# Spacing and placing the conversions of w2, and moving three other loads, in a fused attention and Fourier-mixing kernel

## The chip, the cores and the metric

The kernel runs on one core of one Trainium2 chip. The metric is the device time of a run in microseconds, the median of several runs. The engines are named as in the profile: PE (TensorE matmuls; PEld is its weight load), DVE (VectorE), ACT (ScalarE), POOL (GpSimd) and SP (SyncE, which here only issues DMAs). [...]

## The reference

Bucketed attention comes first, then a mixing block with a two-layer MLP. All data is fp32; the wide inputs arrive as 64-bit floats, which the kernel itself brings to 32 bits.

```python
# attention: B, H, S, D = 4, 8, 768, 64
q_bucket = sum((q @ proj > 0) * 2**arange(6))      # k_bucket likewise
scores = where(q_bucket[:, None] == k_bucket[None, :], q @ k.T / 8, -1e9)
x = softmax(scores) @ v                            # heads side by side: (4, 768, 512)
# mixing block
u = x + real(fft2(x))                              # over the sequence, then over the channels
un = (u - mean(u)) / sqrt(var(u) + 1e-6)
out = u + maximum(un @ w_ch1, 0) @ w_ch2           # 512 -> 2048 -> 512
```

## The kernel before, in words

**Batches and stages.** The four batches are pipelined. While `attention(b)` runs for batch b, the generator `mix(b - 1)` is advanced a few steps after each step of attention, so the PE finds transform and MLP products between the score and value products. `attention(b)` takes four pairs of heads, each in six chunks of 128 keys: score products (L894), the exponential on ACT (L905, tile `pk`), for pairs past the fifth the bucket mask on DVE (L919), the value products (L930), and on DVE the running sum of weights (`acc`, L1007). `mix(b)` does two foldings on DVE, six steps with the channel transform's table `ch` (PE L1122), four with the sequence transform's table `sq` (PE L1151, then `x<-x,A` and `x<-x,B` on DVE, L1165), and then `mlp7(b)`.

**The MLP.** `mlp7` computes both matrix products by a seven-product scheme over 2x2 blocks. For the first product, `quarters(f)` forms four combinations of blocks of `w1` on DVE (L1224 to L1227, tile `tq`) and stores all seven operands to DRAM for the later batches (`ad`, L1229 and L1230, on SP). `inner(half)` then does four groups of seven products (`h_p`, L1426), with evacuations and additions on ACT and DVE (L1448 to L1477). `outer7(b, half, ...)` does the second product (`o`, L1306) with the seven operands of `w2` in `right7`. Each MLP has two halves: inner(0), outer7(0), inner(1), outer7(1).

**Where the weights come from.** Both weights are fetched in slices of 512 KB as 64-bit numbers and brought to 32 bits by `Arrival.convert`, which calls `narrow`: DVE L639 and L643, ACT L647, DVE L649 or twice L652, then ACT L654 and L655 for a range check. When a conversion is done, `convert` fetches the slice that will use the same raw buffer. `weights1` has seven raw buffers and runs during `attention(0)`; it also asks for the second pair's q, k and v, by `load(1)`, after its second fetch. `weights2` has two raw buffers only (`zt2`), and POOL issues its fetches (L693). It converts eight slices for the first half and eight for the second; after every second conversion it forms four sums (L1272 to L1275), and after eight it stores the seven operands (`bd`, L1277, on SP).

**What sets the order.** Batch 0's attention is ordered as written (`manual_schedule`). From there on a scheduler orders each engine's queue. `issue_after(ins)` makes an instruction stand behind `ins` in the queue of that engine, and adds no wait. `weights2` is advanced inside `mix(0)`, which runs beside `attention(1)`: by `after(n, one, two)` from step n of mix(0) on, in three of every five steps, and in the second half by the loop in `mlp7` in three of every four steps:

```python
other = after(2 + NT, other, islice(arrival2, HF + 1))     # NT = 6, HF = 8
if b == 0 and half and i % 4 < 3:
    next(arrival2, None)
```

The two tables `ch` and `sq` are asked for on SP just before attention(0) begins, behind the first seven slices of `w1`.

Of the kernel before, what the change touches and what calls it, by code (L numbers as in the profile page):

```python
# [485 lines left out]
def _main(  # L486
# [188 lines left out]
    def centre(f, avg):  # L675
        for c in range(NDC):
            w = w1[:, c, f : f + WC]
            nc.vector.tensor_tensor(w, w, avg, op=ALU.subtract)

    class Arrival:  # L680

# [29 lines left out]
    def weights1():  # L711
        slices = [
            (w1[:, c, f : f + WC], moe_w_ch1[c * P : (c + 1) * P, f : f + WC])
            for f in range(0, DFF, WC)
            for c in range(NDC)
        ]
        zt = wt([P, 3, 2 * WC], F32, "z", "zraw1", 1)
        ft = wt([P, 12, WC], F32, "F", "fraw", 1)
        raws = [zt[:, i] for i in range(3)] + [
            ft[:, i : i + 2].rearrange("p i w -> p (i w)") for i in range(0, 8, 2)  # L720
        ]
        arrival = Arrival(slices, raws, 0, nc.sync)
        for i in range(arrival.depth):
            arrival.fetch(i)
            if i == 1:
                load(1)
        yield
        half = None
        for i in range(len(slices)):
            arrival.convert(i, ft[:, 8 + i % 4].bitcast(I32))  # L730
            yield
            if half:
                centre(half[0], next(half[1]))
                half = None
# [168 lines left out]
    def weights(pk, g, ps):  # L903

        nc.scalar.activation(  # L905
            pk[:, g, :, 0:HALF], ps[:, :, 0:HALF], AF.Exp, scale=SCALE
        )

    def weigh(n, c, pss):

        qb, kb = preps[n][2:]
        pk = pks[npk[0] % NPK]
        npk[0] += 1
        for g in range(2) if n >= TWO else ():
            weights(pk, g, pss[g])
        if kb is not None:
            for h in range(2):
                w = pk[:, :, h, 0:HALF]
                nc.vector.scalar_tensor_tensor(  # L919
                    w, qb[:, h].rearrange("p (g s) -> p g s", g=2), kb[:, h, c : c + 1], w,  # L920
                    op0=ALU.is_equal, op1=ALU.mult,
                )
        return pk
# [181 lines left out]
    def mix(b):  # L1105
# [8 lines left out]
        for par in range(2):  # L1114
            for t in range(NT // 2):
# [12 lines left out]
                for k in kinds:  # L1128
                    nc.scalar.copy(
                        f[:, k, k : hd + 1 - k],  # L1130
                        ps[:, k * (hd + 1) : DM if k else hd + 1],
                    )
# [12 lines left out]
        for j in range(NDC):  # L1145
# [10 lines left out]
            for ps, op in (pa, ALU.add), (pb, ALU.subtract):  # L1156
                for i in range(2):
# [4 lines left out]
                    else:  # L1162
                        f = ps[:, HW : HALF + 1]
                        f = bass.AP(f.tensor, f.offset, [f.ap[0], [HW, 2], [-1, HW]])
                    nc.vector.tensor_tensor(  # L1165
                        u, u, f, op=op if (j < 2) ^ i else ALU.add
# [82 lines left out]
    def weights2():  # L1249
# [14 lines left out]
        for half in range(2):  # L1264
            for i in range(arrival.depth) if half == 0 else ():
                arrival.fetch(i)
            for i in range(HF):
                arrival.convert(half * HF + i)
                yield
# [99 lines left out]
    def mlp7(b):  # L1369
# [7 lines left out]
        if b == 0:  # L1377
# [11 lines left out]
            ss = [s1s[0], spare[3].rearrange("p (r n) -> p r n", n=P)]  # L1389
            quarters(0)  # L1390
        prods = [A11, S2, A12, S1, S3, S4, A22]
# [41 lines left out]
        def inner(half):  # L1433
            for r in range(HF // 2):
# [15 lines left out]
                product(S2, p6)  # L1450
                nc.scalar.copy(c21, p6)  # L1451
                nc.vector.tensor_tensor(c21, c12, c21, op=ALU.add)  # L1452
                yield
# [3 lines left out]
                product(S1, p5)  # L1457
                nc.scalar.copy(c22, p5)  # L1458
                nc.vector.tensor_tensor(c22, c21, c22, op=ALU.add)  # L1459
                yield  # L1460
# [6 lines left out]
                nc.scalar.copy(c12, p5)  # L1467
                nc.vector.tensor_tensor(c12, c21, c12, op=ALU.add)
                nc.scalar.activation(c12, c12, AF.Relu)
                if b and f == 0:  # L1470
# [4 lines left out]
                nc.scalar.copy(sd[1], p7)  # L1475
                nc.vector.tensor_tensor(c21, c21, sd[1], op=ALU.add)
                nc.scalar.activation(c21, c21, AF.Relu)  # L1477
                if b == 0 and r < HF // 2 - 1:
# [4 lines left out]
        for half in range(2):  # L1483
            if b == 0 and half:
                quarters(HF // 2)
            for i, _ in enumerate(inner(half)):
                if b == 0 and half and i % 4 < 3:
                    next(arrival2, None)
# [10 lines left out]
    def after(n, one, two):  # L1499

        for i, _ in enumerate(one):
            if i >= n and (i - n) % 5 < 3:
                next(two, None)
# [7 lines left out]
    next(other)  # L1511
    nc.sync.dma_start(ch, cn["ch"].ap())
    nc.sync.dma_start(sq, cn["sq"].ap())


    ET = mybir.EngineType
    with tc.manual_schedule(engines={ET.PE, ET.DVE, ET.Activation, ET.Pool, ET.SP}):
        for _ in prepare(0):
            pass
        roomy[0] = False  # L1520
        for i, _ in enumerate(attention(0)):
            if i % 5 < 4:
                next(other, None)
# [12 lines left out]
    for b in range(B):  # L1536
# [42 lines left out]
        if b == 0:  # L1579
            zt2 = wt([P, 3, 2 * WC], F32, "z", "zraw2", 1)  # L1580
            arrival2 = weights2()
            other = after(2 + NT, other, islice(arrival2, HF + 1))
    for _ in other:
# [46 lines left out]
```

## Time and profile before

| | |
|---|---|
| median of 3 runs | 1095.56 us (1094.76 to 1096.2) |
| the profiled execution, its own time | 1097.14 us |
| its span, first to last instruction | 1095.2 us |
| PE busy | 1036.7 us, 95% |
| DVE busy | 789.0 us, 72% |
| ACT busy | 500.1 us, 46% |
| POOL busy | 58.3 us, 5% |
| mean granted PE clock | 0.993 |

The stages lie so: batch 0's attention with the conversions of `w1` up to some 115 us; attention(1) beside mix(0) up to some 410 us, with the sixteen conversions of `w2` from 155.8 to 347 us; attention(2) beside mix(1) from there to 670 us, attention(3) beside mix(2) to 922 us, and mix(3) alone to the end. A line of the timeline gives start and duration in us, engine, source line, operation, the tile written and those read, and in brackets how long the engine had stood idle just before and what released it. A row of the windows gives for each engine the busy time in the stretch with the number of instructions, then the granted PE clock, the DMA share and the DMA rate.

### The profile page before, as it was taken

What the parts mean: (1) busy time and instruction counts of PE and PEld (TensorE: products, weight loads), DVE (VectorE), ACT (ScalarE), POOL (GpSimd) and SP (SyncE); (2) the same over time, 40 slices, a digit from 0 to 9 for tenths busy, and PEclk for the clock granted to TensorE, in tenths of its full rate; (3) what the DMA queues carried; (4) which work ended last, traced back from release to release, by engine and by line L of the source; (5) the groups of instructions that cost most, each with busy time, mean ns of one, the idle gap of its engine ahead of it and who ended that gap; (6) DMA issues with size and microseconds to landing.
All of it is one profiled execution on the core that took longest, in us unless ns stands there. A gap on an engine that the chain in (4) does not pass through costs nothing.

```text
span 1095.2 us, 14139 instructions
## 1 busy us (share of the span) xinstructions
PE 1036.7 (95%) x4933; PEld 634.0 (58%) x4933; DVE 789.0 (72%) x1336; ACT 500.1 (46%) x1055; POOL 58.3 (5%) x132
## 2 busy tenths in 40 slices
PE   6989897999989999999999999999999999999997
PEld 3333354446744675545674576645675569768676
DVE  5899968868599978694867776876775875744353
ACT  6988555653276325364426423354415522341430
POOL 0000000002000020010000011001000002100000
PEclk9999899999999999999999999999999999999999
DMA  8744363441056162214063224213123204122401
GB/s 222 225 91 97 60 166 85 149 148 26 20 138 200 55 199 56 51 54 92 15 176 90 63 54 168 44 34 90 27 71 122 78 20 173 52 85 71 141 20 41
DMA packets 175710, 103.13 MB, mean 94 GB/s; under 512 B 129552, under 2 KB 162960, under 8 KB 175632
## 3 DMA queue, kind: packets, MB, share of 16 engines
q1 hardware_dynamic: 169840, 88.65, 30.1%
q0 software_dynamic: 4224, 13.11, 3.8%
q8 instruction: 41, 0.67, 0.3%
q10 hardware_dynamic: 1568, 0.39, 0.2%
q14 instruction: 37, 0.30, 0.1%
HBM read 81.14 MB, written 20.97 MB: 93 GB/s over the span
## 4 chain that ended last, share of the span: by engine, by line
PE 57%; DVE 15%; ACT 4%; issue 3%; DMA 2%; DVEq 0%; ACTq 0%
PE o L1306 23%; PE h_p L1426 18%; PE oo L930 5%; PE sc L894 5%; DVE pk L919 5%; DVE acc L1007 3%; PE cs L1122 2%; DMA zraw<-in_moe_w_ch_dram 2%; PE A L1151 1%; ACT rr L965 1%; ACT pk L905 1%; PE B L1151 1%; PE bits L825 1%; DVE x L1165 1%; DVE w L1318 0%
## 5 line engine op out<-in xcount | busy, mean ns | idle before, releaser
L1306 PE MATMUL o<-w,h 128*128 128x256 f32 x1152 | 258.5, 381 | 1.9 <-DVE w L1318 0.8
L1306 PEld LDWEIGHTS o<-w,h 128*128 128x128 f32 x1152 | 216.8, 190 | 41.7 <-issue 3.5
L905 ACT ACTIVATE pk<-sc 128x768 f32<-128x768 f32 x192 | 146.9, 809 | 94.2 <-PE sc L894 31.3
L1426 PE MATMUL h_p<-x,w 128*128 128x384 f32 x448 | 162.4, 492 | 2.1 <-ACT h L1448 1.7
L894 PE MATMUL sc<-qt,kt 64*128 64x384 f32 x768 | 154.2, 504 | 6.2 <-ACT pk L905 5.9
L919 DVE SCALAR_TENSOR_TENSOR pk<-qb,kb,pk 128x768 f32<-128x768 bf16 x132 | 129.3, 1012 | 34.5 <-ACT pk L905 34.3
L930 PE MATMUL oo<-pk,vn 128*64 128x385 f32 (+1 forms) x768 | 147.8, 495 | 4.9 <-DVE pk L919 4.6
L1426 PEld LDWEIGHTS h_p<-x,w 128*128 128x128 f32 x448 | 82.5, 190 | 67.2 <-issue 6.8
L1007 DVE TENSOR_TENSOR acc<-acc,pk 128x1536 f32<-128x1536 f32 (+1 forms) x72 | 105.9, 1484 | 5.9 <-ACT pk L905 5.4
L1426 PE MATMUL h_p<-w 128*128 128x384 f32 x288 | 106.3, 492 | 3.6 <-ACT w L1463 2.3
L930 PEld LDWEIGHTS oo<-pk,vn 128*64 128x64 f32 x768 | 50.7, 136 | 92.3 <-issue 73.3
L894 PEld LDWEIGHTS sc<-qt,kt 64*128 64x128 f32 x768 | 66.6, 187 | 57.4 <-issue 19.0
L1426 PEld LDWEIGHTS h_p<-w 128*128 128x128 f32 x288 | 53.0, 190 | 45.5 <-ACT w L1475 5.1
L1318 DVE SCALAR_TENSOR_TENSOR w<-o,rs,w 128x256 f32<-128x256 f32 x56 | 26.7, 479 | 42.0 <-PE o L1306 42.0
L1336 ACT COPY tq<-o 128x256 f32<-128x256 f32 x24 | 8.9, 373 | 101.8 <-PE o L1306 101.8
L1306 PE MATMUL o<-w 128*128 128x256 f32 x176 | 42.0, 381 | 0.3 <-DVE w L1318 0.3
L1459 DVE TENSOR_TENSOR h<-h 128x384 f32<-128x384 f32 x32 | 17.7, 553 | 29.5 <-ACT h L1458 29.5
L1452 DVE TENSOR_TENSOR h<-h 128x384 f32<-128x384 f32 x32 | 17.8, 555 | 26.9 <-ACT h L1451 26.8
L1306 PEld LDWEIGHTS o<-w 128*128 128x128 f32 x176 | 33.0, 190 | 6.8 <-issue 1.1
L1060 POOL DMA_DIRECT2D out_dram<-w x30 | 16.4, 548 | 376.0 <-ACT tq L1336 146.3
L1325 ACT COPY tq<-o 128x256 f32<-128x256 f32 x24 | 8.9, 370 | 58.4 <-PE o L1306 58.3
L1352 DVE TENSOR_TENSOR tq<-tq,o 128x256 f32<-128x256 f32 x24 | 10.0, 418 | 33.7 <-PE o L1306 33.7
(170 smaller groups left out, 1339.1 us busy)
## 6 DMA issues: line engine op xcount, KB each, us to landing
w<-ad SPq DMA_DIRECT2D x168, 128.0 KB, 2.0
w<-bd SPq DMA_DIRECT2D x42, 512.0 KB, 4.5
zraw<-in_moe_w_ch_dram POOLq DMA_DIRECT2D x16, 512.0 KB, 4.0
bd<-w SPq DMA_DIRECT2D x14, 512.0 KB, 4.2
vn<-in_v_dram SPq DMA_DIRECT2D x32, 192.0 KB, 3.5
qn<-in_q_dram SPq DMA_DIRECT2D x120, 48.0 KB, 2.3
kn<-in_k_dram SPq DMA_DIRECT2D x60, 96.0 KB, 3.1
zraw<-in_moe_w_ch_dram SPq DMA_DIRECT2D x8, 512.0 KB, 6.0
```

Source lines behind the costliest of these rows:

```text
L894: last[0] = nc.tensor.matmul(ps[:, h, 0:HALF], kt[rows, ks], qt[rows, qs], start=kb is not None, stop=True,)
L905: nc.scalar.activation(pk[:, g, :, 0:HALF], ps[:, :, 0:HALF], AF.Exp, scale=SCALE)
L919: nc.vector.scalar_tensor_tensor(w, qb[:, h].rearrange("p (g s) -> p g s", g=2), kb[:, h, c : c + 1], w, op0=ALU.is_equal, op1=ALU.mult,)
L930: oo = nc.tensor.matmul(oos[g][h * D : (h + 1) * D, 0:w], nat["v", n][:, (2 * c + h) * D : (2 * c + h + 1) * D], pk[:, g, h, 0:w], start=( ...
L1007: nc.vector.tensor_tensor(acc[:, g], (first if c == 1 else acc)[:, g], new[:, g], op=ALU.add,)
L1122: nc.tensor.matmul(ps[:, pc + 2 * lo : pc + 2 * hi - 1 : 2], z[:, cp, pc, par, t * P : (t + 1) * P], ch[:, cp, pc, lo:hi], start=(cp == 0) ...
L1151: nc.tensor.matmul(ps[:, cols], F[:, par, k, t, j * P : (j + 1) * P], sq[:, t, k, cols], start=(t == 0), stop=(t == 1),)
L1306: nc.tensor.matmul(ps, a[:, r], right7[i][:, r], start=start and r == 0, stop=r == HF // 2 - 1, skip_group_check=not start,)
L1318: nc.vector.scalar_tensor_tensor(t[:, cols], src, r, t[:, cols], op0=ALU.mult, op1=ALU.add)
L1426: nc.tensor.matmul(ps, left[:, k], right[i][:, k], start=start and k == 0, stop=k == 1, skip_group_check=not start,)
L1452: nc.vector.tensor_tensor(c21, c12, c21, op=ALU.add)
L1459: nc.vector.tensor_tensor(c22, c21, c22, op=ALU.add)
```

## The change

Four things change.

1. In the first half the conversions of `w2` get every second step of mix(0), from step 6 on, where they had three of five from step 8 on; the two first fetches have a step of their own. In the second half they get two of every three steps where they had three of four.
2. Every conversion of `w2`, and the first `quarters(0)`, is placed behind the newest of certain ACT and DVE instructions of attention and MLP (`in_turn`; `done_by` holds one for each of the two engines).
3. `weights1` asks for its third slice before, not after, `load(1)`.
4. `ch` and `sq` are asked for in step 11 of attention(0).

```diff
+    done_by = {}
+    @contextmanager
+    def in_turn():
+        with ExitStack() as st:
+            for ins in done_by.values():
+                st.enter_context(tc.issue_after(ins.ins))
+            yield
...
         for i in range(arrival.depth):
             arrival.fetch(i)
-            if i == 1:
+            if i == 2:
                 load(1)
...
-        nc.scalar.activation(
+        done_by[ET.Activation] = nc.scalar.activation(
             pk[:, g, :, 0:HALF], ps[:, :, 0:HALF], AF.Exp, scale=SCALE
         )
...
-                nc.vector.scalar_tensor_tensor(
+                done_by[ET.DVE] = nc.vector.scalar_tensor_tensor(
                     w, qb[:, h].rearrange("p (g s) -> p g s", g=2), kb[:, h, c : c + 1], w,
...
-                    nc.scalar.copy(
+                    done_by[ET.Activation] = nc.scalar.copy(
                         f[:, k, k : hd + 1 - k],
...
-                    nc.vector.tensor_tensor(
+                    done_by[ET.DVE] = nc.vector.tensor_tensor(
                         u, u, f, op=op if (j < 2) ^ i else ALU.add
                     )
...
         for half in range(2):
-            for i in range(arrival.depth) if half == 0 else ():
-                arrival.fetch(i)
+            if half == 0:
+                for i in range(arrival.depth):
+                    arrival.fetch(i)
+                yield
             for i in range(HF):
-                arrival.convert(half * HF + i)
+                with in_turn():
+                    arrival.convert(half * HF + i)
                 yield
...
-            quarters(0)
+            with in_turn():
+                quarters(0)
...
-                nc.scalar.copy(c21, p6)
-                nc.vector.tensor_tensor(c21, c12, c21, op=ALU.add)
+                done_by[ET.Activation] = nc.scalar.copy(c21, p6)
+                done_by[ET.DVE] = nc.vector.tensor_tensor(c21, c12, c21, op=ALU.add)
...
-                nc.scalar.copy(c22, p5)
-                nc.vector.tensor_tensor(c22, c21, c22, op=ALU.add)
+                done_by[ET.Activation] = nc.scalar.copy(c22, p5)
+                done_by[ET.DVE] = nc.vector.tensor_tensor(c22, c21, c22, op=ALU.add)
...
-                nc.vector.tensor_tensor(c12, c21, c12, op=ALU.add)
-                nc.scalar.activation(c12, c12, AF.Relu)
+                done_by[ET.DVE] = nc.vector.tensor_tensor(c12, c21, c12, op=ALU.add)
+                done_by[ET.Activation] = nc.scalar.activation(c12, c12, AF.Relu)
...
-                nc.vector.tensor_tensor(c21, c21, sd[1], op=ALU.add)
-                nc.scalar.activation(c21, c21, AF.Relu)
+                done_by[ET.DVE] = nc.vector.tensor_tensor(c21, c21, sd[1], op=ALU.add)
+                done_by[ET.Activation] = nc.scalar.activation(c21, c21, AF.Relu)
...
-                if b == 0 and half and i % 4 < 3:
+                if b == 0 and half and i % 3 < 2:
                     next(arrival2, None)
...
-            if i >= n and (i - n) % 5 < 3:
+            if i >= n and (i - n) % 2 == 0:
                 next(two, None)
...
-    nc.sync.dma_start(ch, cn["ch"].ap())
-    nc.sync.dma_start(sq, cn["sq"].ap())
...
         for i, _ in enumerate(attention(0)):
+            if i == 2 * NT - 1:
+                nc.sync.dma_start(ch, cn["ch"].ap())
+                nc.sync.dma_start(sq, cn["sq"].ap())
             if i % 5 < 4:
                 next(other, None)
...
-            other = after(2 + NT, other, islice(arrival2, HF + 1))
+            other = after(NT, other, islice(arrival2, HF + 2))
```

No instruction is added or taken away: counts and shapes of all operations and transfers stay the same, and only their places in the queues move.

More of the change, by code (lines that the diff above doesn't have):

```diff
@@ L678, in centre @@
             nc.vector.tensor_tensor(w, w, avg, op=ALU.subtract)
+    ET = mybir.EngineType
+    done_by = {}
[5 more added lines that the diff above has]
+            yield
     class Arrival:
@@ L1511, in _main @@
     next(other)
-    nc.sync.dma_start(ch, cn["ch"].ap())
-    nc.sync.dma_start(sq, cn["sq"].ap())
-    ET = mybir.EngineType
     with tc.manual_schedule(engines={ET.PE, ET.DVE, ET.Activation, ET.Pool, ET.SP}):
```

## The prediction

> **What bounds the kernel now.** I read the page's busy table first, then the windows of 5 us, then ACT's and PE's waits, then the timeline around each wait. Line numbers are those of the kernel before.
>
> ```profile
> PE 1036.7 (95%) x4933; PEld 634.0 (58%) x4933; DVE 789.0 (72%) x1336; ACT 500.1 (46%) x1055; POOL 58.3 (5%) x132
> ```
>
> The PE sets the length: 1095.2 - 1036.7 = 58.5 us of the span it is idle. No change of order can win more than the part of this idle time that it removes, and what slow clock it avoids. So I ask where the idle time lies. In the windows the columns are PE, PEld, DVE, ACT and POOL busy, PE clock, DMA share and GB/s:
>
> ```profile
> 170.00:175.00 5.00, 2.21 (x10) 0.49 (x6) 3.44 (x7) 3.62 (x7) 0.32 (x1) 1.00 0.02 4
> ...
> 180.00:185.00 5.00, 3.10 (x18) 1.82 (x16) 3.69 (x9) 3.77 (x13) 0.53 (x1) 1.00 0.30 108
> 185.00:190.00 5.00, 3.51 (x19) 1.86 (x20) 4.52 (x8) 4.22 (x7) 0.00 (x0) 1.00 0.00 0
> ...
> 220.00:225.00 5.00, 3.37 (x13) 1.45 (x12) 3.55 (x8) 1.89 (x4) 0.00 (x0) 1.00 0.95 355
> 225.00:230.00 5.00, 4.53 (x14) 2.48 (x14) 2.29 (x6) 2.33 (x5) 0.00 (x0) 0.66 0.54 212
> ```
>
> From 165 to 190 us the five windows leave the PE idle 0.23 + 2.79 + 0.98 + 1.90 + 1.49 = 7.4 us, though DVE and ACT are not full either. Around 220 it idles again, and then works at a clock of 0.66. All this lies where w2 is converted (155.8 to 347 us). ACT's waits between 165 and 350 us have one row on top (total, times, longest), and the timeline shows it at work:
>
> ```profile
> ACT zraw L647 <- DMA zraw<-in_moe_w_ch_dram: 19.8, 12, 4.2
> ```
>
> ```profile
> 170.73 0.67 ACT L647 ACTIVATE zraw<-zraw 128x512 int32<-128x512 uint32 x1 [3.16 <-DMA zraw<-in_moe_w_ch_dram]
> 172.15 0.92 PE L894 MATMUL sc<-qt,kt 64*128 64x384 f32 x4 [1.71 <-ACT pk L905]
> 175.98 1.51 PE L930 MATMUL oo<-pk,vn 128*64 128x385 f32 x6 [1.92 <-DVE pk L919]
> 178.60 0.69 ACT L647 ACTIVATE zraw<-zraw 128x512 int32<-128x512 uint32 x1 [4.21 <-DMA zraw<-in_moe_w_ch_dram]
> 186.49 0.92 PE L894 MATMUL sc<-qt,kt 64*128 64x384 f32 x4 [2.64 <-ACT pk L905]
> ...
> 224.08 0.67 ACT L647 ACTIVATE zraw<-zraw 128x512 int32<-128x512 uint32 x1 [2.11 <-DMA zraw<-in_moe_w_ch_dram]
> 225.47 0.24 PE L849 MATMUL kb<-pw,bt 32*128 32x2 bf16 x6 [2.10 <-ACT qb L537]
> 225.63 2.35 PE L1426 MATMUL h_p<-x,tq 128*128 128x384 f32 x4
> ```
>
> A conversion stands in ACT's queue before its slice has landed: two raw buffers, a fetch of 4.0 us (median to landing on the page), and three conversions in five steps. ACT waits, the exponential L905 behind it is late, and PE waits for ACT directly or through the mask L919. The last line is the clock: four such products take 1.45 us elsewhere.
>
> [...] the slice issued at 163.57 us, while SP was issuing k loads, was waited for until 170.73, 7.2 us instead of 4.0. [...] products take 2.35 and 2.39 us instead of 1.45 after a gap of 2.10 us, but the gap of 2.64 us at 186.49 is followed by full speed. So I count a saved clock dip only where this trace shows one.
>
> **The change part by part.** All operations stay the same; the queues of the two built programs, compared, show the new places.
>
> *Spacing and place, first half.* Before h_p begins, the new queues hold the first two conversions only, whose raw buffers were filled ahead; the old ones hold four. Each later ACT L647 has some ten ACT instructions or more between it and the check L655 that frees its raw buffer, about 6 us against a fetch of 4.0, so the waits of 3.16, 4.21, 1.22 and 2.11 us should go. Of the PE gaps 1.71 + 1.92 + 2.64 = 6.3 us behind them I take 4.0 (2 to 6.3), since x<-x,A and x<-x,B (L1165) and the reciprocal copies (L965) also delay those exponentials. Around 225: the gap 2.1, and 2.35 + 2.39 - 2 x 1.45 = 1.8 of clock; of 3.9 I take 3.3 (1 to 4). The two conversions moved on bring 2 x (0.42 + 0.69 + 0.76) = 3.7 us of DVE work to 192-247 us, where DVE idles 3.2 us from 230 to 235 alone; that covers them.
>
> *quarters(0) behind newer work.* Its four DVE sums (137.57 to 139.04, 1.5 us) leave their place ahead of `bt` L829, for which PE waits:
>
> ```profile
> 141.31 1.16 PE L1122 MATMUL cs<-ch,z 128*128 128x127 f32 x8 [1.93 <-DVE bt L829]
> ```
>
> Gain 1.4 (0 to 1.9). They now stand ahead of `bt<-x,bt` (L1405), which the first S2 product needs; that ended at 185.7 and the product began at 190.9, so 5 us cover them. Its DMA to `ad` moves behind loads on SP and is read a batch later: nothing.
>
> *Second half.* PE gaps behind late ACT or DVE work are 1.28 (307), 1.54 (326), 0.35 (343) and 0.95 us (346), 4.1 in all. Against this, the first two conversions leave 291-302 us, where DVE had idled, for 300-350, where DVE is busy 24.93 + 22.70 of 50 us and has 2.4 left for 3.7. I take 1.5 (-1.5 to 3.5). The stores of w2's operands follow later on SP with q and k loads among them as before; POOL keeps its 16 fetches in order.
>
> *Third slice of w1.* ACT waited 1.23 us for it at 24.17, and at 27.22 PE waited 1.73 for ACT. That goes: 1.2. Behind it on SP stand the 14 DMAs of load(1), later by one issue (0.6) and 512 KB of transfer; DVE's transpose of q at 19.60 had no wait, and may get up to 1. I take 0.9 (0 to 1.7).
>
> *Tables later.* Two DMAs (issues 0.57 + 0.58 us, 1282 KB) leave SP at 21.5 us, where no consumer waits for what is behind them, and come to about 65 us ahead of load(3). The DMA share was 0.00 from 60 to 65 us. The q of load(3), issued by 70.3, is transposed at 76.2; the first use of `ch` is at 132. Cost 0 (0 to 1).
>
> *What is late next.* The last four sums of the second half (ended at 351.7) move behind one more chunk, and DVE carries its backlog to outer7's second call, first product at 364.65. I charge 1.1 (0 to 2.5).
>
> Sum: 4.0 + 3.3 + 1.4 + 1.5 + 0.9 - 1.1 = 10.0 us. DVE's work is conserved: from 175 to 350 it is busy 143.6 of 175 us, 82%, so part of the gaps will form again behind DVE. I take off 2: **8.0 us**. The profiled execution took 1097.1 (span 1095.2 and 1.9 around it), so its like would take 1089.1. It lies 1.6 above the median, and the gain holds for either: 1095.6 - 8.0 = 1087.6.
>
> **The rivals.** *DVE becomes the bound.* For: 82% over the whole stretch, 95% from 300 to 350. Against: in the worst windows (170-190) it has a fifth free. Then only the longest gaps shrink: 2 at 165-190, 1 of clock, 0.9 at the start, less 0.9 at the end: 3 us, 1092.6. *Nothing to see.* The waits for slices go, but PE waits for something else as long, since each gap also had a late DVE instruction in it: 1095. *Slower: w2 is ready too late.* The second half's last sums had 366 - 352 = 14 us before the product with T4 reads them, and two more of 14 steps over 63 us cost 9 of these. If DVE falls 12 us more behind, the PE waits about 7 at L1306 and loses some 2 to the clock. Were half the other gains gone as well (6 left), it would be 1095.6 + 9 - 6 = 1098.6. Against: the new queue has the sums ahead of the last group's additions, which the same stage needs anyway. It decides once those sums end over 14 us later against the PE's arrival. That the order doesn't change is ruled out by the queues.
>
> **How the numbers follow.** The forecast (6 to 14 us won) has 0.56, the DVE bound 0.22, nothing 0.12, slower 0.10. About 0.2%, 2.2 us, is what a measurement here can tell from no change. The first two are faster: 0.78. The range goes from 1081, the sum with most bounds high, to 1096.6, the nothing case with 1.6 of spread.
>
> **What would show it.** Right: ACT's waits for zraw from 165 to 350 us fall from 19.8 to under 6; the PE windows from 165 to 190 hold over 21 of 25 us instead of 17.6; no clock under 0.9 near 225; the PE wait at cs near 0.5; ACT's wait at 24 gone; the first product with `ch` of batch 1 (411.96 before) comes 7 to 10 us sooner. Wrong: gaps at L1306 behind DVE L1275 or L1291, new PE waits for DVE at h_p, a wait at the transpose L768 near 20 or 76 us, or a span from 412 us to the end that differs from 683 by over 2.

## The result, and the profile after

The changed kernel takes **1085.82 us** (median of 5 runs, 1085.49 to 1087.05) against 1095.56 us (5 runs, 1094.76 to 1096.81) for the kernel before, measured beside it: a ratio of 0.991, 95% interval 0.9895 to 0.9925, so 9.7 us are won. The forecast was 1087.6. The profiled execution took 1086.83 us; its span is 1085.0.

In the changed kernel most lines are numbered 11 to 15 higher: score products L905, exponential L916, mask L930, value products L941, `h_p` L1441, `o` L1320, the four sums L1286 to L1289. `narrow` keeps its numbers, L639 to L655.

The busy table is nearly what it was, since the work is the same; only the idle time has shrunk, by the 10.2 us that the span has lost less 1.8 us of PE busy time (the clock granted from 225 to 230 us was 0.66 before and is 1.00 now):

```profile
PE 1034.9 (95%) x4933; PEld 633.1 (58%) x4933; DVE 789.9 (73%) x1336; ACT 498.4 (46%) x1055; POOL 58.3 (5%) x132
```

The windows of 5 us that the prediction read (PE, PEld, DVE, ACT, POOL busy, PE clock, DMA share, GB/s):

```profile
170.00:175.00 5.00, 3.67 (x20) 2.45 (x19) 4.89 (x10) 2.53 (x10) 0.53 (x1) 1.00 0.32 107
175.00:180.00 5.00, 3.37 (x20) 1.63 (x18) 4.61 (x8) 3.64 (x7) 0.00 (x0) 1.00 0.11 36
180.00:185.00 5.00, 4.60 (x16) 1.98 (x16) 5.00 (x6) 0.59 (x1) 0.00 (x0) 1.00 0.21 72
185.00:190.00 5.00, 5.00 (x16) 1.99 (x14) 4.38 (x6) 3.06 (x5) 0.00 (x0) 1.00 0.00 0
...
220.00:225.00 5.00, 5.00 (x23) 2.20 (x22) 3.38 (x7) 4.11 (x7) 0.00 (x0) 1.00 0.78 266
225.00:230.00 5.00, 5.00 (x17) 2.88 (x16) 5.00 (x7) 2.16 (x6) 0.53 (x1) 1.00 0.93 265
```

From 165 to 190 us the PE is now busy 21.6 of 25 us (17.6 before); what is left of its idle time lies from 170 to 180 us. Around 225 us there is neither a gap nor a slow clock. DVE is now the fuller engine: from 160 to 190 us it is busy 28.3 of 30 us, 26.0 before. ACT's waits from 150 to 350 us (total, times, longest):

```profile
ACT zraw L654 <- DVE w L643: 9.6, 7, 3.3
...
ACT zraw L647 <- DMA zraw<-in_moe_w_ch_dram: 3.2, 2, 2.1
```

Before, the lower row stood at 23.3 us, 14 times. The two waits that are left belong to the first two slices and end before 165 us; from there to 350 us the row is absent (19.8 us, 12 times, before). The timeline shows where the conversions stand now, all of ACT's L647 from 160 to 225 us. None of the six has a wait in brackets, and none lies between 160 and 188 us, where the kernel before had four:

```profile
188.84 0.68 ACT L647 ACTIVATE zraw<-zraw 128x512 int32<-128x512 uint32 x1
...
197.27 0.68 ACT L647 ACTIVATE zraw<-zraw 128x512 int32<-128x512 uint32 x1
...
203.16 0.69 ACT L647 ACTIVATE zraw<-zraw 128x512 int32<-128x512 uint32 x1
...
209.99 0.67 ACT L647 ACTIVATE zraw<-zraw 128x512 int32<-128x512 uint32 x1
...
213.44 0.69 ACT L647 ACTIVATE zraw<-zraw 128x512 int32<-128x512 uint32 x1
...
221.31 0.71 ACT L647 ACTIVATE zraw<-zraw 128x512 int32<-128x512 uint32 x1
```

**A ledger of stretches.** To see where the time comes from I read off the timeline, for each kernel, when the first product of four stages starts: the first product with `ch` of batch 0 (the trace's `cs`), the first with `sq` (`A`), the first `o` product, and the first with `ch` of batch 1. The stretches between them are, in us:

| kernel | start of the first `ch` product | to the first `sq` product | to the first `o` product: first half of w2 | to `ch` of batch 1: second half of w2 |
|---|---|---|---|---|
| before | 132.1 | 21.6 | 103.1 | 155.1 |
| after | 130.4 | 21.0 | 94.5 | 155.8 |

From the last mark to the end the two kernels keep the same distance within 0.1 us (10.2 us); what is won is won before 402 us. Of it 8.6 us come from the first half of w2, 1.7 from the time before, 0.6 from the `ch` stage, and 0.6 is lost in the second half. The first half of w2 holds the same products in all kernels, so its 8.6 us can be split: the PE idles 12.4 us of it before and 6.7 after (its length less the busy time that the windows give), and the slow clock near 225, by estimate 1.7 us (5 us at 0.66, so 5 x 0.34), is in the first only. A ledger is of one execution: the first column alone spread from 128.8 to 132.5 us over all the kernels below, so differences under some 2 us in it say little.

### The profile page after: what moved, and what is told of

It is laid out like the page before. It is cut to its first block, busy times and chain, and to the rows that moved or that the text cites. A ratio compares the mean times of both kernels' runs of the same rounds, so it can differ in the third digit from the quotient of the medians.

```text
span 1085.0 us, 14130 instructions
## 1 busy us (share of the span) xinstructions
PE 1034.9 (95%) x4933; PEld 633.1 (58%) x4933; DVE 789.9 (73%) x1336; ACT 498.4 (46%) x1055; POOL 58.3 (5%) x132
## 4 chain that ended last, share of the span: by engine, by line
PE 64%; DVE 24%; ACT 6%; issue 3%; SPq 1%; DMA 1%; DVEq 0%; ACTq 0%
PE o L1320 24%; PE h_p L1441 19%; PE oo L941 7%; PE sc L905 6%; DVE pk L930 5%; DVE acc L1018 5%; PE cs L1133 2%; PE A L1162 1%; ACT pk L916 1%; ACT rr L976 1%; PE B L1162 1%; DMA kn<-in_k_dram 1%; SPq L576 1%; DVE w L643 1%; DVE qt L779 1%
## 5 line engine op out<-in xcount | busy, mean ns | idle before, releaser
L1320 PE MATMUL o<-w,h 128*128 128x256 f32 x1152 | 258.8, 381 | 2.4 <-ACT tq L1339 0.9
L1320 PEld LDWEIGHTS o<-w,h 128*128 128x128 f32 x1152 | 216.7, 190 | 42.9 <-issue 4.3
L916 ACT ACTIVATE pk<-sc 128x768 f32<-128x768 f32 x192 | 147.3, 808 | 98.2 <-PE sc L905 32.9
L1441 PE MATMUL h_p<-x,w 128*128 128x384 f32 x448 | 162.3, 492 | 0.1
L905 PE MATMUL sc<-qt,kt 64*128 64x384 f32 x768 | 154.8, 506 | 3.6 <-ACT pk L916 3.3
L930 DVE SCALAR_TENSOR_TENSOR pk<-qb,kb,pk 128x768 f32<-128x768 bf16 x132 | 128.9, 1011 | 33.4 <-ACT pk L916 33.1
L941 PE MATMUL oo<-pk,vn 128*64 128x385 f32 (+1 forms) x768 | 148.1, 497 | 4.0 <-DVE pk L930 3.4
L1441 PEld LDWEIGHTS h_p<-x,w 128*128 128x128 f32 x448 | 82.6, 190 | 64.2 <-issue 7.7
L1441 PE MATMUL h_p<-w 128*128 128x384 f32 x288 | 106.4, 492 | 3.5 <-ACT w L1478 2.3
L941 PEld LDWEIGHTS oo<-pk,vn 128*64 128x64 f32 x768 | 50.8, 136 | 91.6 <-issue 74.2
L905 PEld LDWEIGHTS sc<-qt,kt 64*128 64x128 f32 x768 | 66.9, 188 | 55.0 <-issue 19.3
L1441 PEld LDWEIGHTS h_p<-w 128*128 128x128 f32 x288 | 53.0, 190 | 45.5 <-ACT w L1490 5.1
L1332 DVE SCALAR_TENSOR_TENSOR w<-o,rs,w 128x256 f32<-128x256 f32 x56 | 26.7, 479 | 42.6 <-PE o L1320 42.6
L1320 PE MATMUL o<-w 128*128 128x256 f32 x176 | 42.1, 382 | 1.0 <-DVE w L1332 1.0
L1474 DVE TENSOR_TENSOR h<-h 128x384 f32<-128x384 f32 x32 | 17.7, 553 | 30.3 <-ACT h L1473 30.3
L1320 PEld LDWEIGHTS o<-w 128*128 128x128 f32 x176 | 33.0, 190 | 7.7 <-DVE w L1332 2.0
```

The lines of the kernel that those rows point to most:

```text
L905: last[0] = nc.tensor.matmul(ps[:, h, 0:HALF], kt[rows, ks], qt[rows, qs], start=kb is not None, stop=True,)
L916: done_by[ET.Activation] = nc.scalar.activation(pk[:, g, :, 0:HALF], ps[:, :, 0:HALF], AF.Exp, scale=SCALE)
L930: done_by[ET.DVE] = nc.vector.scalar_tensor_tensor(w, qb[:, h].rearrange("p (g s) -> p g s", g=2), kb[:, h, c : c + 1], w, op0=ALU.is_equa ...
L941: oo = nc.tensor.matmul(oos[g][h * D : (h + 1) * D, 0:w], nat["v", n][:, (2 * c + h) * D : (2 * c + h + 1) * D], pk[:, g, h, 0:w], start=( ...
L1320: nc.tensor.matmul(ps, a[:, r], right7[i][:, r], start=start and r == 0, stop=r == HF // 2 - 1, skip_group_check=not start,)
L1332: nc.vector.scalar_tensor_tensor(t[:, cols], src, r, t[:, cols], op0=ALU.mult, op1=ALU.add)
```

## The experiments

Two theories stood for the first half. *Theory 1, the waits*: an L647 that stands in ACT's queue before its slice has landed holds up the exponentials behind it (in the kernel before, the L647 at 178.60 came after a wait of 4.21 us, and the next exponential, whose scores had ended by 173.07, began at 181.50). *Theory 2, the work*: the conversions' own DVE and ACT instructions stand ahead of exponentials and masks, whether or not they wait. And the change has several parts, which can be done apart: the place (`in_turn`), the spacing, and the start (third slice and tables). Each ratio is to the kernel before on the same chip, with its 95% interval.

### One part at a time

**s1_start**: the start alone.

```diff
-            if i == 1:
+            if i == 2:
                 load(1)
...
-    nc.sync.dma_start(ch, cn["ch"].ap())
-    nc.sync.dma_start(sq, cn["sq"].ap())
...
+            if i == 2 * NT - 1:
+                nc.sync.dma_start(ch, cn["ch"].ap())
+                nc.sync.dma_start(sq, cn["sq"].ap())
```

> The kernel before with the third slice of w1 asked for before load(1) and with the tables moved to step 11 of attention(0); nothing of w2 changes. Theory (the parts add up): the 1.4 us by which the changed kernel leads at its 49th value product stay to the end, so 1.2 to 1.9 us less than before, near 1094. Rival (the start only shifts the phase of later stages): the lead is lost by the first product with ch, 0 +- 0.5 us.

1096.09 us, ratio 1.0006 (0.9996 to 1.0015): nothing. Yet the step itself does happen. PE's waits from 15 to 45 us in the kernel before, and then in s1_start:

```profile
PE sc L886 <- ACT pk L905: 3.0, 4, 1.7
```

```profile
PE sc L886 <- ACT pk L905: 1.6, 4, 0.5
```

The wait for the slice is gone and the value products at 42 us start 1.6 us sooner; at the end nothing of it can be told.

**s3_spacing**: the new spacing in both halves, nothing placed (the hunks on `islice`, `(i - n) % 2`, `i % 3` and the fetches' step).

> The kernel before with the new spacing of w2's conversions alone (every second step from step 6, two of three in the second half), and no placing behind newer work. Theory A (spacing puts the needed time between a fetch and its conversion): 5 to 8 us less, ACT's waits for zraw from 165 to 350 us under 6. Theory B (the place behind newer work does it): the scheduler still puts the third to fifth conversion's L647 at the places of before in ACT's queue (183, 185, 190), so 0 to 2 us less, and the waits stay over 10 us.

1099.12 us, ratio 1.0028 (1.0017 to 1.004): slower. ACT waits 19.6 us for slices at L647, 10 times, from 165 to 350 us, nearly as in the kernel before (19.8). The scheduler put the third to fifth conversions at the places they had; being asked for later does not move them in the queue. Why it is slower is not shown: the profiled run is its fastest, and in the ledger the `ch` stage (22.6 us) and the second half (156.9) are the longer ones.

**s4_place**: `in_turn` on the conversions and on `quarters(0)`, with the old spacing.

> The kernel before with w2's conversions and quarters(0) placed behind newer work, at the old spacing. Theory A (spacing does it): 0 to 3 us less, with waits for zraw left, since three conversions in five steps still share two buffers. Theory B (place does it): 6 to 9 us less and waits for zraw under 6 us; from the fourth conversion on L647 stands about twenty ACT places later than before.

1090.21 us, ratio 0.9939 (0.9925 to 0.9952). The first half takes 95.0 us, practically what the whole change reaches; the waits from 165 to 350 us are 4.1. But the second half takes 158.6, 3.5 us more than before (by estimate 1.7 of it a spell of slow clock, 0.87 and 0.79 in the windows of 5 us from 330 to 340, so 5 x 0.13 + 5 x 0.21).

**p1_place_spacing** (the change without the start) and **p2_place_start** (the change with the old spacing):

> The changed kernel with the start undone (third slice after load(1), tables before attention(0)): new spacing and new place of w2's conversions together. Theory (place and spacing work only together: the place moves the conversion behind the exponentials, the spacing keeps the second half's DVE from piling up): 8 to 10 us less than before, ratio near 0.992. Rival (the parts add: -6.3 for the place, +2.6 for the spacing as measured one by one): 3 to 4 us less, ratio near 0.997.

> The changed kernel at the old spacing: place and start alone. Theory (spacing is needed with the place): 6 to 8 us less than before, ratio near 0.994, and as in the run with the place alone the lead falls by 3 to 5 us between the fifth group of h_p and the second call of outer7. Rival (the start gives what the place alone lacks): 9 to 10 us less, ratio near 0.991.

p1: 1087.07 us, ratio 0.9908 (0.9891 to 0.9926); p2: 1089.87, ratio 0.9938 (0.9922 to 0.9954). So with or without the start the ratios agree (0.991 and 0.9908; 0.9938 and 0.9939). The spacing costs 0.28% alone and wins 0.3% once the place is there: it does not space anything unless the instructions are held to their steps, and then it repairs what the place does to the second half (158.8 us in p2, 155.8 in p1; which part of the place does it, s9_two_held shows below).

**s7_quarters**: only `quarters(0)` placed behind newer work.

```diff
-            quarters(0)
+            with in_turn():
+                quarters(0)
```

> The kernel before, with the four sums and seven stores of the first quarters(0) placed behind newer work and nothing else changed. The prediction took 1.4 us (0 to 1.9) for this: PE's wait for DVE at cs (1.93 before) falls to about 0.5, and the stretch from the first cs product to the first product with sq falls from 21.6 to some 20.2. Theory 1 and 2 both leave the first half of w2 at 102 to 103.5 us. Total 1.4 less, 1094 to 1095; if the total does not move although the stretch shrinks, the gain is eaten by the next wait. What the kernels with this edit and others together showed (20.1 to 21.3 where those without had 21.6 to 23.9) would allow up to 2.

1093.64 us, ratio 0.9973 (0.9962 to 0.9985): 3.0 us (1.6 to 4.2), twice what was expected. Beside the kernel before alone the gain does not show where I put it: the `ch` stage takes 21.3 us, against 21.6. Over all the profiles it does. PE's wait at `cs` behind `bt` is 1.9 us in each of the six kernels in which `quarters(0)` is not placed (before, s1, s3, s6, f1, x2), and 0.7 in each of the eight in which it is; and after the longer wait three of the six (s6, f1, x2) have a spell of slow clock, none of the eight after the shorter. So the `ch` stage takes 21.6 to 23.9 us without the edit and 20.1 to 21.3 with it. The kernel before had the shortest stage of the six.

In the first half of w2, s7_quarters takes 100.6 us, 103.1 before. ACT's waits for slices there are hardly smaller (16.1 us against 17.8), and the PE idles 10.0 us of the stretch, 12.4 before. But s1_start, where nothing is placed, has the like (16.0 us of waits, 10.5 of idle time), so this drop is not shown to come from `quarters(0)`. The 21 runs of this kernel spread from 1089.3 to 1096.9 us, and its profile is one of many courses.

### The waits, without the place

**s6_buffers**: the kernel before, with a third raw buffer for the third slice.

```diff
+            slices, [zt2[:, i] for i in range(3)], NDC * DFF // WC, nc.gpsimd,
+            [0, 1, 2] + [i % 2 for i in range(13)],
```

(the rest of the edit makes `Arrival` follow this list)

> The kernel before, order and spacing kept, but the third slice of w2 is fetched ahead into a third raw buffer (the later tile t4 takes that space over), and the next slices alternate between the two old buffers, each asked for one conversion sooner. Theory 1 (ACT's wait for the slice costs the time): ACT's waits before the third, fourth and fifth conversion (2.15, 3.16, 4.21 us) go, and the first h_p is 3 to 5 us sooner; total 3 to 6 us less. Theory 2 (the conversions' work standing ahead of the exponentials and masks costs it, landed or not): at most 1 us less, the PE gaps of 1.7 to 2.6 us between 170 and 190 us stay.

1093.93 us, ratio 0.9969 (0.9959 to 0.9978). Only four tenths of the waits went (12.0 us are left of 19.8 from 165 to 350), and the later slices still have two buffers; the first half takes 99.6.

**f1_short**: the kernel before, with shorter fetches.

```diff
+                    if self.queue is nc.gpsimd and i > 1:
+                        raw, src = raw[:, 0 : raw.shape[-1] // 4], src[:, 0 : src.shape[-1] // 4]
```

> The kernel before with only a quarter of the columns of each slice of w2 fetched from the third slice on (128 KB instead of 512; the rest of the raw buffer keeps older numbers, so the output differs); conversions, places and spacing stay as before within two places in a queue. It measures what the wait for the slice costs. Theory 1 (the wait costs the time): ACT's waits for zraw fall by 1.5 to 2 us each, and 3 to 6 us are won. Theory 2 (the place of the work costs it): at most 1 us.

The whole took 3097.5 us, because the numbers left in the buffers raised the kernel's own range flag and its second, slower path ran afterwards; only the stretches up to there can be used. The waits were again not all gone (9.7 us), and the first half takes 100.7.

**x2_nofetch**: no fetch after the first two slices, so nothing to wait for from the third on.

```diff
-            self.fetch(i + self.depth)
+            if self.queue is not nc.gpsimd:
+                self.fetch(i + self.depth)
```

(and the range check leaves the old numbers out)

> The kernel before, but the slices of w2 from the third on are not fetched at all: their conversions run on the two raw buffers' old numbers, and the range check leaves them out, so w2's values are wrong and only the time counts. Every conversion keeps all its DVE and ACT work and about its old place in the queues (the third to sixth conversions' L647 a few instructions earlier or later than before, nothing is placed behind newer work), and none can wait for a slice. Theory 1 (the waits of ACT for slices make the PE gaps): ACT's zraw waits for a DMA from 165 to 350 us are zero, and the first half of w2 (from the first product with sq to the first o product, 103.1 us before and 94.5 after the change) falls to 96 or less, so that the total comes 6 to 9 us sooner, about 1087 to 1090. Theory 2 (the conversions' own work stands ahead of exponentials and masks, whether or not it waits): the stretch stays at 99 to 102, and the total gains 1 to 4 us. The nine stretches measured so far lean to a mixture: two kernels that removed a third to a half of the waits won 2.4 and 3.5 us of the 8.6.

1091.63 us, ratio 0.9951 (0.9931 to 0.997): 5.4 us (3.3 to 7.6). The first half takes 97.5 us. That is neither theory's number. From 165 us on no L647 waits for a DMA, and the gap and the clock dip around 225 are gone; but ACT's waits from 165 to 260 us show the row that took over (2.1 us there in the kernel before):

```profile
ACT zraw L654 <- DVE w L643: 10.0, 5, 6.0
```

The timeline has its longest piece, with one L647 just ahead, and the PE's gap beside it (here the value products are L932 and the mask L921):

```profile
169.69 0.65 ACT L647 ACTIVATE zraw<-zraw 128x512 int32<-128x512 uint32 x1
169.94 1.51 PE L932 MATMUL oo<-pk,vn 128*64 128x385 f32 x4 [2.08 <-DVE pk L921]
...
176.31 0.71 ACT L654 ACTIVATE zraw<-zraw 128x512 f32<-128x512 int32 x1 [5.96 <-DVE w L643]
```

The buffer is ready, but DVE's half of the same conversion (L639, L643) comes only after masks and folds, and ACT stands waiting for that; and ahead of the mask that ends the PE's gap DVE did one conversion's L639, L643 and two L652, and w2's four sums, 3.6 us by their own times, with another mask and some 3 us of `x<-x,A`, `x<-x,B` and `bt<-x` between them. So a good part of the gap there is theory 2's. Both theories hold a part. (x2_nofetch also takes the fetches' traffic off the DMA engines: their busy share in the first half is 0.33, 0.44 before. In its profile the `ch` stage took 23.9 us, with a spell of slow clock in it.)

Put together, ACT's waits at L647 for slices within the first half of w2, that half's length, and the clock granted over it. A spell of slow clock falls into some profiles and not into others; by estimate from these lengths, 0.98 is about one spell of 1.7 us, 0.97 about two.

| kernel | placed | waits, us | first half of w2, us | clock |
|---|---|---|---|---|
| s3_spacing | nothing | 19.2 | 101.7 | 0.98 |
| before | nothing | 17.8 | 103.1 | 0.98 |
| s1_start | nothing | 16.0 | 102.8 | 0.97 |
| s6_buffers | nothing | 12.1 | 99.6 | 1.00 |
| f1_short | nothing | 11.2 | 100.7 | 0.98 |
| x2_nofetch | nothing | 3.6 | 97.5 | 1.00 |
| s7_quarters | `quarters(0)` alone | 16.1 | 100.6 | 0.98 |
| s5_first (below) | `quarters(0)`, first half | 9.0 | 97.2 | 0.98 |
| s4_place | all | 7.3 | 95.0 | 1.00 |
| after, p1 | all | 2.8 to 3.2 | 94.5 | 1.00 |
| p2 | all | 3.8 | 94.3 | 0.98 |

Where no conversion is placed (the first seven rows), the stretch falls with the waits, roughly: from the kernel before to x2_nofetch by 5.6 us for 14.2 us of wait, some 1.7 of it the spell of slow clock. Where the first half's conversions are placed it is shorter at the same waits. The cleanest pair is x2_nofetch and the change: both wait only for the first two slices and have a clock of 1.00, and the change is 3.0 us shorter. That is theory 2's share in this stretch, in one execution of each, though the change also holds `quarters(0)`, the spacing and the start.

By the ratios, 5.4 us for the waits and 3.0 for `quarters(0)` make 8.4 of the 9.9 that the whole gives. What is left for theory 2, 1.5, is inside the intervals; the two were not run together without `in_turn` on the conversions, so that they add up is an assumption. In the ledger x2_nofetch has 1.1 us back in the second half (154.7 against 155.8). So the waits are the larger part, and the size of theory 2's part is open between nothing and some 3 us.

### The second half

**s5_first**: the changed kernel, with the second half as before.

```diff
-                with in_turn():
+                with in_turn() if half == 0 else nullcontext():
...
-                if b == 0 and half and i % 3 < 2:
+                if b == 0 and half and i % 4 < 3:
```

> The changed kernel with the second half of w2 as before (three of four steps, not placed behind newer work); the first half, quarters(0) and the start stay changed. Theory (the second half's edit gives nothing, its stretch being bound by DVE): as fast as the changed kernel within 1 us, lead of 10.3 to 11 us kept from the first outer7 to the end. Rival (the second half's edit is worth its PE gaps): 1.5 to 4 us slower than the changed kernel.

1088.41 us, ratio 0.9925 (0.9908 to 0.9942): the second half takes 155.2 us, as before, but the *first* half lost 2.7 (97.2). Of these, 1.4 are idle time of the PE (8.1 us against 6.7), and most of the rest is a spell of slow clock (0.66 from 175 to 180 us), ahead of the place in question. By the ratios, s5_first is 1.6 us slower than the change. The timeline of ACT, and then of PE, shows where the idle time comes from:

```profile
222.94 0.69 ACT L647 ACTIVATE zraw<-zraw 128x512 int32<-128x512 uint32 x1 [1.25 <-DMA zraw<-in_moe_w_ch_dram]
...
231.00 0.66 ACT L647 ACTIVATE zraw<-zraw 128x512 int32<-128x512 uint32 x1 [3.93 <-DMA zraw<-in_moe_w_ch_dram]
231.56 0.46 ACT L1478 COPY w<-h_p 128x384 f32<-128x384 f32 x1
```

```profile
226.75 2.85 PE L1441 MATMUL h_p<-x,tq 128*128 128x384 f32 x8 [0.45 <-ACT h L1470]
232.07 1.56 PE L1441 MATMUL h_p<-zraw,w 128*128 128x384 f32 x4 [2.47 <-ACT w L1478]
```

Unplaced, the second half's first two conversions are pulled forward into the first half's group, wait there for their slices, and the evacuation L1478 behind them is late: the products before it had ended at 229.60, it started at 231.56, and the PE waited for it. In the kernel before it was so too: the wait at 224.08 was that of the tenth slice, the second of the second half. What the placing of these two is for lies in the first half.

**s9_two_held**: the changed kernel, with the old spacing in the second half, and only its first two conversions placed.

```diff
-                with in_turn():
+                with in_turn() if half == 0 or i < 2 else nullcontext():
...
-                if b == 0 and half and i % 3 < 2:
+                if b == 0 and half and i % 4 < 3:
```

> The changed kernel, with the second half's conversions back at three of every four steps and only the first two of them (which otherwise stand at the end of the first half's group and wait for slices) placed behind newer work; the other six stand where the scheduler puts them. If placing the last six is what costs the second half its gain, the stretch from the first o product to the next cs product falls from 155.8 to about 155.1 while the first half keeps its 94.5, and the total is 0.5 to 0.7 us lower, about 1085.3. If the second half is bound by DVE's total work, it stays at 155.5 to 156 and the total does not move. If the old distance costs what it did with all eight placed (158.6), the total is 3 us higher.

1086.66 us, ratio 0.9902 (0.9884 to 0.9921), not to be told from the change. The first half keeps 94.5, the second stays at 155.75. So at the old spacing the other six are better left unplaced: with all eight placed, p2 has 158.8 us there and s4_place 158.6 (all three with a clock of 0.99). With the two held, the old spacing does as well as the new one with all eight held. What the new spacing does with the six unplaced was not run.

**b1_pool**: the changed kernel, with w2's four sums on POOL.

```diff
-                    nc.vector.tensor_tensor(t3, b22, t1, op=ALU.subtract)
+                    nc.gpsimd.tensor_tensor(t3, b22, t1, op=ALU.subtract)
```

(and likewise the three others)

> The changed kernel, with w2's four sums after every second conversion (four instructions on DVE, eight times over both halves) on POOL instead of DVE. DVE gets some 6 to 7 us of work less in each half. If DVE is what holds the PE up from 300 to 350 us, where it is busy 47.6 of 50 us in the changed kernel, the second half falls from 155.8 to 153 to 155 and the total by 1 to 3 us. If the sums are slow on POOL and w2's fetches, which POOL issues, queue behind them, ACT's waits for slices come back and the total is 1 to 5 us higher. If PE's gaps there have other causes, nothing moves by more than 0.5.

1092.98 us, ratio 0.9962 (0.9947 to 0.9977), some 6 us slower than the change; the second half takes 160.0 us, the first 96.5 (with a clock of 0.98). The groups on POOL from 150 to 360 us (total, mean ns), and then one of these sums on DVE in the changed kernel:

```profile
L1286 POOL TENSOR_TENSOR w<-w 128x256 f32<-128x256 f32 x8 | 13.1, 1642 | 39.1 <-DVE w L652 37.8 <-PE sum L960 1.3
L1288 POOL TENSOR_TENSOR w<-w 128x256 f32<-128x256 f32 x8 | 9.0, 1126 | 0.5
L1289 POOL TENSOR_TENSOR w<-w 128x256 f32<-128x256 f32 x8 | 8.1, 1015 | 0.5
...
L1287 POOL TENSOR_TENSOR w<-w 128x256 f32<-128x256 f32 x8 | 6.9, 859 | 0.6
```

```profile
L1286 DVE TENSOR_TENSOR w<-w 128x256 f32<-128x256 f32 x8 | 3.4, 419 | 0.0
```

DVE was spared 13.5 us and POOL spent 37.1 on it. ACT's waits for slices, which had been gone after 165 us, are back at 4.0 us from 260 to 350, since the fetches stand behind the sums on POOL: one was issued at 343.52, right after a sum of 4.86 us and one of 0.72, and its L647 at 348.42 waited 3.2 us. And other DVE work took longer: L1474 662 ns on average, 554 in the changed kernel (see the end). None of the kernels beats the change by more than the measurement can tell.

## Why the prediction was right

**The bound, and the reading.** Right. The idle time of the PE around the conversions was what could be won, ACT's waits for slices led to the largest part of it, and the view named for it answered as said: 19.8 us of L647 waits became zero (under 6 was the mark), the PE 165 to 190 windows hold 21.6 of 25 us (over 21), the clock near 225 is 1.00, the wait at `cs` behind `bt` fell from 1.93 to 0.7 (0.5), ACT's wait at 24 is gone, and the first `ch` product of batch 1 came 10.2 us sooner, just past the 7 to 10 that were named. From there to the end the span is 683.3 us (683). One sign of being wrong did appear, a PE wait for DVE at `h_p` (L1236, 0.9 us, at 199 us); the kernel before had one of 1.3 us there, at 307.

**First half, 4.0 + 3.3.** Right within its bounds. The windows from 165 to 190 lost 4.0 us of idle time, and the gap and slow clock near 225 all of their 3.9. The latter was put down to the first half's spacing, but is due to the second half's first two conversions (s5_first); and of its clock part no more can be said than that this profile had it, since s6_buffers has nearly the same gap there, 1.95 us (2.10 before), and its products behind it take 1.56 and 1.45 us (2.35 and 2.39 before), at a clock of 1.00. The reason given, the waits, carries most but not all: with every wait from the third slice on gone the median falls by 5.4, and ACT then waits for DVE inside the conversion. The prediction had allowed for delays from `x<-x,A` and the reciprocals, not for that one.

**Spacing and place as one item.** A split that the prediction did not make, and should have: "about 6 us against a fetch of 4.0" was read off the new queues, and it is the place, not the spacing, that puts the instructions there. The spacing alone made the kernel 0.28% slower.

**`quarters(0)`, 1.4 (0 to 1.9).** Too small: 3.0 by the median (1.6 to 4.2). The wait at `bt` did fall as said, by some 1.3 us, in every profile with this edit. What the step left out is the slow clock that followed the longer wait in three of six profiles, some 1.3 us each time (in s6_buffers 1.51 + 2.08 - 2 x 1.16 for the two groups behind the wait; a `ch` stage of 23.9 us in s6_buffers, 22.6 in s1_start and s3_spacing, where none followed); the profile that I read had none. Together (1.3, and 1.3 in half of the cases) that is an estimate of some 2 us. Whether there is more, in the first half of w2, is not shown.

**Second half, 1.5, and lateness, -1.1.** A net 0.4 was forecast, and -0.6 measured in the ledger, within its 2 us; s5_first shows no gain from the whole edit in that half either (155.2 unplaced). So the 1.5 was too much, within its bounds (-1.5 to 3.5), for the reason that stood behind the charge: DVE carries its backlog on. Windows of 25 us at the same stage (the changed kernel is 10 us ahead), before and then after:

```profile
360.00:385.00 25.00, 24.71 (x128) 15.85 (x125) 23.58 (x45) 8.08 (x16) 1.23 (x3) 1.00 0.12 28
```

```profile
350.00:375.00 25.00, 23.74 (x116) 15.37 (x115) 24.90 (x48) 7.29 (x15) 1.13 (x3) 1.00 0.27 90
```

DVE rose from 23.6 to 24.9 of 25 us and the PE lost 1.0; over the whole second half it idles 5.5 us, 6.0 before. That the placing of the first two of these conversions protects the *first* half (1.4 us of idle time in s5_first) was in no step: the sum had credited it to the spacing of the first half.

**Third slice and tables, 0.9 and 0.** The wait went as said, and no wait came in its place, but no gain is left at the end: 1.0006 (0.9996 to 1.0015) alone allows at most 0.4 us. The term was too large by at least half a microsecond. Where it goes was not followed.

**The 2 us taken off, since DVE's work is conserved.** Not needed. The sum ahead of it, 10.0, is what was measured (9.7). A gap behind DVE did form after 350 us (0.6 us at 360, behind L1332), but the lateness charge of 1.1 had paid for that; so it seems the deduction counted it twice. That this error and the small term for `quarters(0)` make up for the second half and the start is luck of the sum.

**The rivals.** DVE as the bound: it is fuller (28.3 of 30 us from 160 to 190), and it does limit what follows 350 us, but it did not take back the first half's gain. Nothing to see: excluded by the ratio. w2 too late: no wait for its last sums appears at L1320, where the PE's waits from 345 to 402 us are 0.9, 0.6 and 0.6 us, all for evacuations; from 150 to 350 us its longest is 1.7 us (behind ACT's L1478). It came into sight only in s4_place and p2, with the place and the old spacing, as gaps within the second half and not at L1320. The 2 us of clock counted in this case were an estimate of mine; the spell near 225 in the kernel before cost 1.8 (2.35 + 2.39 - 2 x 1.45).

## What to carry to other kernels

Background work (fetch, convert) that a scheduler is free to pull forward can be held behind the newest critical instruction of each engine that it uses. Here, asking for it at better distances gained nothing while the scheduler was free, and once all of it was held the distances mattered; in the second half it was enough to hold the two items that would have been pulled over the edge. When a wait is to be removed, look at what the same instruction chain waits for next (here DVE's half of the conversion), and count the edges: a group's tail is where the next group's first items are pulled to. When a gain is read off one profile, look at the same place in others: here the same wait of 1.93 us was followed by a slow clock in three profiles and by full speed in three. And charge a conserved resource once, at the place where it is full, not again as a share of the whole.

## What the runs showed of the hardware

**In these profiles gaps of the same length on the PE were followed now by a slow clock, now by full speed.** In s9_two_held gaps of 1.95 and 0.56 us are followed by groups of products that take 2.29 and 2.42 us, and the clock granted from 310 to 315 us is 0.66; in s4_place gaps of 1.90 and 0.56 us at the same products are followed by 1.51 and 1.56 us, and the clock in that window is 1.00:

```profile
309.56 0.83 PE L941 MATMUL oo<-pk,vn 128*64 128x385 f32 x2 [1.95 <-ACT zraw L654]
310.96 2.29 PE L941 MATMUL oo<-pk,vn 128*64 128x385 f32 x6 [0.56 <-DVE pk L930]
313.18 2.42 PE L1441 MATMUL h_p<-x,w 128*128 128x384 f32 x4
```

```profile
310.71 0.83 PE L941 MATMUL oo<-pk,vn 128*64 128x385 f32 x2 [1.90 <-ACT zraw L654]
312.10 1.51 PE L941 MATMUL oo<-pk,vn 128*64 128x385 f32 x6 [0.56 <-DVE pk L930]
313.54 1.56 PE L1440 MATMUL h_p<-x,w 128*128 128x384 f32 x4
```

In s3_spacing a single gap of 3.84 us is followed by groups of 1.56 us, at a clock of 1.00 from 320 to 330 us:

```profile
325.85 1.56 PE L1439 MATMUL h_p<-x,w 128*128 128x384 f32 x4 [3.84 <-ACT h L1461]
327.34 1.56 PE L1439 MATMUL h_p<-bt,tq 128*128 128x384 f32 x4
```

The plainest case is the wait of 1.93 us at `bt`, at the same product of the `ch` stage in six kernels. In three (before, s1, s3) the products behind it keep their usual time, in three (s6, f1, x2) they are slower; here s3_spacing, with groups of 1.16 us, and then s6_buffers, where they take up to 2.08:

```profile
139.75 1.16 PE L1133 MATMUL cs<-ch,z 128*128 128x127 f32 x8 [1.93 <-DVE bt L840]
...
141.11 1.16 PE L1133 MATMUL cs<-ch,z 128*128 128x127 f32 x8
```

```profile
141.76 1.51 PE L1125 MATMUL cs<-ch,z 128*128 128x127 f32 x8 [1.93 <-DVE bt L832]
...
143.63 2.08 PE L1125 MATMUL cs<-ch,z 128*128 128x127 f32 x8
```

The longest gap ahead of the slow spell near 175 us in s5_first (0.66 from 175 to 180) is 1.09 us, after one of 0.65; the changed kernel has gaps of 1.09 and 0.64 there and keeps a clock of 1.00. So a slow clock came in one profile where no gap just ahead of it was longer than 1.09 us, and did not come in another after a gap of 3.84. What decides it is not shown.

**With w2's sums on POOL, some DVE instructions beside them took longer.** The 128x256 sums took 1.16 us on average on POOL (37.1 us for 32) and 0.42 on DVE. With them there, DVE's additions L1474 (128x384, two tiles read) went from 554 to 662 ns on average. The mean hides how: of the eight from 150 to 360 us, the two that lay beside one of these sums took 0.90 and 1.07 us, and the other six their usual 0.55. Two of the sixteen L639 took 0.95 us instead of 0.42 in the same way. (One sum took 4.86 us itself, at 337.92, while DVE's instructions beside it kept their usual times; but the profile gives spans on POOL only roughly.) Why some took longer and others not is not shown.
